# Attention and a two-layer network: item counts per group from a table, operand sums behind the next maximum, a reordered tail

## The chip, the cores and the metric

The kernel runs on one core of a Trainium2 chip. Inputs and outputs lie in the chip's main memory. The metric is the device time of one execution in microseconds (us). A profile of one execution is taken beside it; TensorE ran at its full granted clock in it (1.0).

## The reference

Eight batches, twelve heads, 448 positions, head size 64; then a network of width 768 and inner width 2048. In short:

```python
q_n, k_n = rmsnorm(q, g_q), rmsnorm(k, g_k)          # over the head size
scores = matmul(q_n, k_n^T) / sqrt(64)
attn = exp(scores - max); attn = attn / (sum(attn) + 1e-9)
x = matmul(attn, v)      # -> (8*448, 768)
h = x @ w_in             # (768, 2048)
g = maximum(0.01*h, h)
out = g @ w_out          # (2048, 768)
```

## The kernel before, in words

**Units and quarters.** Attention is cut into 24 units (`u` = 0 to 23): one batch and four of its heads, so three units make a batch. From unit 3 on the main loop has four quarters in each unit (`d` = 0 to 3). A quarter begins with the scores of one or two of the seven key tiles (`qk`, line 199; tile 0 in quarter 0, two tiles in the others) and their exponential on ScalarE (`ex`, line 218). Then `fill(u, d, jobs)` issues some items of the network, which are held in a list `queue`, and the quarter's jobs (loads, squares, normalisation of a later unit, products).

**The head of a unit.** In quarter 0, after the scores of tile 0, VectorE takes their maximum (line 236) and puts it on a diagonal (`dg`, line 238). TensorE does the values product of the unit before (`pv`, line 367, 28 matmuls), its row sums (`zcol`, line 307, 16 to 28 matmuls) and a small matmul that spreads the maxima over the partitions (`shift_mm`, line 248). A second maximum on VectorE (line 249) and line 257 give the bias `eb` of the exponential. ScalarE then copies the values product out (`x`, line 322) and takes the exponential of tile 0. Scores and values product share two slots of PSUM (`sT`): the scores of quarter 1 go into the slot that the exponential of tile 0 has read, and the values product goes into the slot of the last tile of the unit before, after its exponential.

**The row sums' way.** The row sums' logarithm and its exponential (lines 327 and 332) give the reciprocals `zs`, which four transfers on SP's queue spread (`rz`, line 337). The product `xt` of `x` and `rz` (line 347) is made by VectorE in some units and by GpSimd in others (8, 9, 12, 14, 15, 18, 20, 21, 22).

**The network.** `push(b)` adds the items of batch `b` to `queue` once its attention is nearly done. `moe1` is one block of 128 inner columns, six matmuls (line 389), with the activation on ScalarE into `gt` (line 383). The second layer has plain items (`moe2`, line 430: 16 inner blocks into one bank, in two parts of eight matmuls, for half the columns of a tile) and items that make two tiles at once from seven products instead of eight (`seven`, items `i0` to `i6`, line 471, eight matmuls of 384 columns each). The seven products need sums of blocks of `gt` (`s1` to `s4`, lines 452 to 461, into `sa`) and of the weights (`tw`). Their banks are called `ma`, `mb`, `mc`, `md`; merges on VectorE (lines 478 and 487) and copies on ScalarE (line 498) put them together, and `i5` and `i6` add a second product to `mc` and `md`. In batches 6 and 7 part of the first layer is made with seven products too (`late1`, lines 591 to 608).

**What is put off.** An item puts the work on its result into the list `pend` (by `later`), and the next item, or the end of `fill`, issues it (`flush`). So the order of each engine's instructions is written by hand, but for the number of items in each quarter: `fill` works that out from costs of items (`queue[i][0]`) and weights of quarters (`WD`), with the rest carried over in `debt`. After each item one job is issued.

**The tail.** After unit 23 come its row sums and values product, the reciprocals (lines 353 and 354) and two products `xt` (line 376), one for each half `r`; then the rest of the items, among them all of batch 7's. VectorE's order there comes from `pend` too.

Of the kernel before, what the change touches and what calls it, by code (L numbers as in the profile page):

```python
# [18 lines left out]
def kernel(  # L19
# [13 lines left out]
    B, H, S, D = q.shape  # L33
# [378 lines left out]
    pend = []  # L412
    L, R, LR = slice(0, HC), slice(HC, DM), slice(0, DM)

    def flush():
        while pend:
            pend.pop(0)()

    def out_tile():
        return opool.tile([P, DM], FP32, tag="ost", name="ost")  # L420

    def moe2(pair, t, half, part):
        flush()
        if half == 0 and part == 0:
            ost[0] = out_tile()
        if part == 0:
            ost[1] = aux([P, 512], FP32, "op2")
        op2 = ost[1]
        for ft in range(8 * part, 8 * part + 8):
            nc.tensor.matmul(op2[:, 0:HC], gt[:, ft, ds(col(t), P)], wout16[:, ft, ds(HC * half, HC)],  # L430
                             start=(ft == 0), stop=(ft == FT - 1))
        if part == 0:
            return
        nc.vector.tensor_copy(ost[0][:, ds(HC * half, HC)], op2[:, 0:HC])
        drop(op2)
        if half == 1:
            store(pair, t, ost[0], LR, False)

    def wblock(i, j):
        return wout16[:, HF * i:HF * i + HF, HC * j:HC * j + HC]  # L440
# [7 lines left out]
    def gblock(t, j):  # L448
        return gt[:, HF * j:HF * j + HF, ds(col(t), P)]
# [11 lines left out]
        nc.vector.tensor_tensor(sa[:, 3, x], gblock(tt[0], 1)[:, x], sa[:, 1, x], op=ALU.subtract)  # L461

    def later(fn, *args):
        pend.append(lambda: fn(*args))

    def seven(pair, tt, nxt=None, last=False):
        g = {}

        def mm(bank, a, b, first):
            for f in range(HF):  # L470
                nc.tensor.matmul(bank[:, 0:HC], a[:, f], b[:, f], start=(first and f == 0), stop=(f == HF - 1), skip_group_check=not first)  # L471

        def bank(name):
            g[name] = aux([P, 512], FP32, name)
            return g[name]

        def add(dst, src, name):
            nc.vector.tensor_tensor(dst, g[name][:, 0:HC], src, op=ALU.add)

        def put(i, c):  # L480
            store(pair, tt[i], g["o"][i], c, last)

        def i0():
            flush()
            g["o"] = (out_tile(), out_tile())
            mm(bank("ma"), gblock(tt[0], 0), wblock(0, 0), True)
            later(lambda: nc.vector.tensor_copy(g["o"][1][:, L], g["ma"][:, 0:HC]))

        def i1():
            flush()  # L490
            mm(bank("mb"), sa[:, 1], tw[:, 1], True)
            later(lambda: add(g["o"][1][:, L], g["o"][1][:, L], "mb"))
            later(lambda: drop(g["mb"]))

        def i2():
            flush()
            mm(g["ma"], gblock(tt[0], 1), wblock(1, 0), False)
            later(lambda: nc.scalar.copy(g["o"][0][:, L], g["ma"][:, 0:HC]))
            later(lambda: drop(g["ma"]))
            if last:  # L500
                later(put, 0, L)

        def i3():
            flush()
            mm(bank("mc"), sa[:, 0], tw[:, 0], True)
            later(lambda: add(g["o"][1][:, R], g["o"][1][:, L], "mc"))
            if nxt:
                later(s1, nxt)

        def i4():  # L510
            flush()
            mm(bank("md"), sa[:, 2], tw[:, 2], True)
            later(lambda: add(g["o"][1][:, R], g["o"][1][:, R], "md"))
            if last:
                later(put, 1, R)

        def i5():
            flush()
            mm(g["mc"], sa[:, 3], wblock(1, 1), False)
            if nxt:  # L520
                later(s2, nxt)
            later(lambda: add(g["o"][0][:, R], g["o"][1][:, L], "mc"))
            later(lambda: drop(g["mc"]))
            later(put, 0, R if last else LR)
            if nxt:
                later(s3, nxt)
                later(s4, nxt)

        def i6():
            flush()  # L530
            mm(g["md"], gblock(tt[1], 1), tw[:, 3], False)
            later(lambda: add(g["o"][1][:, L], g["o"][1][:, L], "md"))
            later(lambda: drop(g["md"]))
            later(put, 1, L if last else LR)

        return [i0, i1, i2, i3, i4, i5, i6]
# [42 lines left out]
    def late1(b, tail, after):  # L579
# [45 lines left out]
        def item(n, s):  # L625
            flush()
            if not g:
                start()
            if n == 1:
                mm(get(1, s), 1, s, x_b(b, 0, 0), True)  # L630
                later(lambda: copy(tmp["u"][:, s % 2], g[1, s][:, 0:S]))
            elif n == 2:
                mm(get(2, s), 2, s, x_b(b, 1, 0), True)
                later(lambda: vadd(tmp["u"][:, s % 2], g[2, s], tmp["u"][:, s % 2]))
                later(lambda: drop(g[2, s]))
                later(lambda: out_(s, 0, 0, tmp["u"][:, s % 2]))
            elif n == 7:
                mm(get(7, s), 7, s, xs[3], True)
                later(lambda: nc.vector.tensor_copy(tmp["v"][:, s % 2], g[7, s][:, 0:S]))
            elif n == 6:  # L640
                mm(g[1, s], 6, s, xs[2], False)
                later(lambda: vadd(g[7, s][:, 0:S], g[1, s], tmp["v"][:, s % 2]))
            elif n == 5:
                mm(g[1, s], 5, s, xs[1], False)
                later(lambda: vadd(tmp["v"][:, s % 2], g[1, s], tmp["v"][:, s % 2]))
                later(lambda: out_(s, 1, 1, tmp["v"][:, s % 2]))
            elif n == 4:
                mm(g[7, s], 4, s, xs[4], False)
                later(lambda: out_(s, 1, 0, g[7, s][:, 0:S]))
                later(lambda: drop(g[7, s]))  # L650
            else:
                mm(g[1, s], 3, s, x_b(b, 1, 1), False)
                later(lambda: out_(s, 0, 1, g[1, s][:, 0:S]))
                later(lambda: drop(g[1, s]))
            for fn in after.get((n, s), ()):
                pend.append(fn)

        return item

# [14 lines left out]
    def push(b):  # L674
# [24 lines left out]
                    items.append((0.575, lambda w=w: item(*w)))  # L699
        if odd:  # L700
            tt, tn = (3, 4), (5, 6)
            items += [(1.31, fn) for fn in seven(pair, tt, tn)]
            for n, x, fs in ((len(items) - 7, 1, (s3, s4)),) if late else ((8, 0, (s1, s2)), (10, 0, (s3, s4)), (FT - 1, 1, (s1, s2)), (FT, 1, (s3, s4))):
                c, fn = items[n]
                items[n] = (c, also(fn, *[lambda f=f, x=x: later(f, tt, half[x]) for f in fs]))
            items += [(1.31, fn) for fn in seven(pair, tn, None, b == B - 1)]
        else:
            tiles = (2,) if fast else (0, 1, 2)
            std = [lambda t=t, h=h, p=p: moe2(pair, t, h, p) for t in tiles for h in range(2) for p in range(2)]
            if fast:  # L710
                tt = (0, 1)
                std[0] = also(std[0], lambda: later(s1, tt), *[lambda: later(win_sum, 3, 0)] * late)
                std[1] = also(std[1], lambda: later(s2, tt))
                std[2] = also(std[2], lambda: later(s3, tt), lambda: later(s4, tt))
                std += seven(pair, tt)
            items += [(1.31, fn) for fn in std]
        queue.extend(items)

    WD = (3.6, 2.9, 2.8, 2.8)
    STEPS = ((0,), (1, 2), (3, 4), (5, 6))  # L720
    debt = [0.0]

    def narrow(u):
        return 4 <= u < NU - 1
# [1 line left out]
    def fed(u, d):  # L726
        return u % NQ == 0 and d == 3

    def fill(u, d, jobs):
        total = sum(c for c, _ in queue)  # L730
        left = WD[d] + 3.0
        uu, dd = u, d
        while True:
            dd += 1
            if dd == 4:
                uu, dd = uu + 1, 0
            if uu == NU or (fed(uu, dd) and (u > 3 or uu > 3)):
                break
            left += WD[dd]
        debt[0] += total * WD[d] / left  # L740
        while queue and debt[0] >= queue[0][0] * 0.5:
            c, fn = queue.pop(0)
            fn()
            debt[0] -= c
            if jobs:
                jobs.pop(0)()
        flush()
        for job in jobs:
            job()

# [20 lines left out]
    with tc.manual_schedule():  # L771
# [190 lines left out]
        for u in range(3, NU):  # L962
            for d in range(4):
                if d > 0 or u > 3:
                    qk(u, STEPS[d])
                    if d == 0:
                        shift_max(u)
                        if u == 6:
                            xmul_sb(u - 2)
                        if narrow(u - 1):  # L970
# [82 lines left out]
        zsum_slot(NU - 1)  # L1053
        pv(NU - 1)
        zinv(NU - 1)
        xmul(NU - 1)
        for i, ns in enumerate(((3, 1), (2, 4))):
            c, fn = queue[i]
            queue[i] = (c, also(fn, *[lambda n=n: later(x_sum, B - 1, n) for n in ns]))
        push(B - 1)  # L1060
        while queue:
            queue.pop(0)[1]()
# [29 lines left out]
```

## Time and profile before

| | us |
|---|---|
| median of 3 runs | 417.51 (416.79 to 417.85) |
| the profiled execution | 417.04 |
| its span | 415.2 |
| TensorE matmuls busy (3817) | 399.3 |
| VectorE busy | 307.7 |
| ScalarE busy | 300.7 |
| GpSimd busy | 68.4 |

A line of the timeline gives start and duration in us, the engine, the line of the kernel, the operation, output and input, and how many like it follow each other. In square brackets stand the idle time of the engine before it and what ended it. PE is TensorE, DVE VectorE, ACT ScalarE, POOL GpSimd, SP the queue of transfers. A line of the waits gives who waited for whom, the total, how often, and the longest.

### The profile page before, as it was taken

The page shows a single profiled execution, that of the slowest core. Times are in us where ns is not written, and L with a number is a line of the kernel's source. Part 1 is how long each engine was busy: PE and PEld are TensorE (multiplying, and loading weights), DVE is VectorE, ACT ScalarE, POOL GpSimd, SP SyncE. Part 2 cuts the span into 40 slices and gives each one's busy share as a digit, 9 for nine tenths or more (in the row PEclk, how much of TensorE's full clock was granted, in tenths as well). Part 3 has the DMA queues.
Part 4 walks back from the last instruction along what each step waited for, and adds up shares of the span by engine and source line. Part 5 has one row for each costly group of instructions (what it writes and reads, how often), then busy time and mean ns, then how long its engine had stood idle before and what let it go on. Part 6 is the DMA issues. An engine that isn't in the chain of part 4 may idle for free.

```text
span 415.2 us, 9343 instructions
## 1 busy us (share of the span) xinstructions
PE 399.3 (96%) x3817; PEld 219.1 (53%) x3817; DVE 307.7 (74%) x492; ACT 300.7 (72%) x470; POOL 68.4 (16%) x70
## 2 busy tenths in 40 slices
PE   8688999999999999999999999999999999999995
PEld 7444444554445544554445544454445557558863
DVE  5888898898788757867669757767669788557762
ACT  5898887677987699867987679867986657653600
POOL 1868432200020200010020200020001202000000
PEclk9999999999999999999999999999999999999999
DMA  6999999999565986678664896678552460032023
GB/s 207 259 255 253 240 249 141 229 174 207 138 154 92 224 213 125 150 173 182 155 155 72 220 196 136 170 147 185 158 103 47 120 160 8 10 75 77 2 55 98
DMA packets 71950, 62.41 MB, mean 150 GB/s; under 512 B 36324, under 2 KB 67044, under 8 KB 71908
## 3 DMA queue, kind: packets, MB, share of 16 engines
q1 hardware_dynamic: 61312, 49.62, 47.3%
q0 software_dynamic: 10272, 11.80, 18.3%
q8 instruction: 30, 0.49, 0.5%
q10 hardware_dynamic: 324, 0.39, 0.3%
q14 instruction: 12, 0.10, 0.1%
HBM read 45.61 MB, written 11.01 MB: 136 GB/s over the span
## 4 chain that ended last, share of the span: by engine, by line
PE 82%; DVE 9%; ACT 6%; issue 2%; DVEq 0%
PE hps L389 27%; PE sT L199 8%; PE sT L367 5%; PE ma L471 5%; PE op L430 5%; PE md L471 5%; PE bank L591 4%; PE mc L471 4%; PE bank L471 4%; ACT et L218 3%; PE mb L471 3%; PE zc L307 2%; DVE n L171 2%; PE warm L769 2%; PE sT L471 2%
## 5 line engine op out<-in xcount | busy, mean ns | idle before, releaser
L218 ACT ACTIVATE et<-sT,eb 128x896 f16<-128x896 f32 x166 | 159.4, 1008 | 26.7 <-PE sT L199 17.4
L389 PE MATMUL hps<-xt,win 128*128 128x448 f16 x600 | 121.0, 353 | 0.3 <-DVE xt L376 0.2
L389 PEld LDWEIGHTS <-win 128*128 128x128 f16 x612 | 56.8, 98 | 58.4 <-issue 10.0
L383 ACT ACTIVATE gt<-hps 128x448 f16<-128x448 f32 x100 | 53.9, 554 | 7.4 <-PE hps L389 6.4
L199 PE MATMUL sT<-qkT 64*64 64x448 f16 x664 | 52.5, 363 | 4.2 <-ACT et L218 2.8
L159 DVE TENSOR_REDUCE ssq<-sq 128x14 f32<-128x896 f32 (+2 forms) x49 | 50.1, 1059 | 0.6 <-ACT sq L148 0.6
L471 PEld LDWEIGHTS <-sa 128*128 128x128 f16 x352 | 32.8, 98 | 26.3 <-issue 6.1
L128 POOL DMA_DIRECT2D vt<-in_v_dram x24 | 17.9, 746 | 172.0 <-PE sT L367 165.2
L471 PEld LDWEIGHTS <-gt 128*128 128x128 f16 x264 | 25.2, 98 | 19.3 <-issue 2.8
L199 PEld LDWEIGHTS <-qkT 64*64 64x64 f16 x672 | 15.4, 104 | 37.3 <-issue 32.6
L322 ACT COPY x<-sT 128x896 f32<-128x896 f32 x16 | 14.5, 906 | 26.0 <-DVE sT L249 26.0
L347 POOL TENSOR_TENSOR xt<-x,rz 128x896 f16<-128x896 f32 x9 | 18.9, 2097 | 80.3 <-DMA rz<-zs 80.3
L171 DVE TENSOR_TENSOR n<-rq,rinv 128x896 f16<-128x896 f32 (+2 forms) x25 | 27.0, 1084 | 5.0 <-ACT rinv L165 5.0
L292 DVE TENSOR_TENSOR ea<-ea,et 128x896 f16<-128x896 f16 x27 | 16.9, 625 | 16.7 <-ACT et L218 15.7
L367 PE MATMUL sT<-et,vt 64*64 64x448 f16 x532 | 28.5, 349 | 0.3
L430 PE MATMUL op<-wout,gt 128*128 128x384 f16 x160 | 28.4, 326 | 0.0
L236 DVE TENSOR_REDUCE sT<-sT 128x1 f32<-128x896 f32 x22 | 24.1, 1094 | 3.6 <-PE sT L199 3.5
L367 PEld LDWEIGHTS <-vt 64*64 64x64 f16 x672 | 20.5, 107 | 11.3 <-issue 1.4
L171 DVE TENSOR_TENSOR n<-rk,rinv 128x896 f16<-128x896 f32 (+2 forms) x26 | 26.1, 1012 | 0.0
L430 PEld LDWEIGHTS <-gt 128*128 128x128 f16 x192 | 17.6, 98 | 14.4 <-issue 3.1
L471 PE MATMUL ma<-wout,gt 128*128 128x384 f16 x128 | 23.5, 326 | 0.0
L292 DVE TENSOR_TENSOR ea<-et 128x896 f16<-128x896 f16 x14 | 9.4, 673 | 11.8 <-ACT et L218 11.7
(144 smaller groups left out, 549.0 us busy)
## 6 DMA issues: line engine op xcount, KB each, us to landing
rq<-in_q_dram SPq DMA_DIRECT2D x24, 448.0 KB, 4.0
rk<-in_k_dram SPq DMA_DIRECT2D x24, 448.0 KB, 5.5
out_dram<-ost SPq DMA_DIRECT2D x52, 192.0 KB, 3.1
rz<-zs SPq DMA_DIRECT2D x76, 112.0 KB, 2.3
vt<-in_v_dram POOLq DMA_DIRECT2D x24, 224.0 KB, 4.8
win<-in_moe_w_in_dram POOLq DMA_DIRECT2D x8, 384.0 KB, 15.8
wout<-in_moe_w_out_dram POOLq DMA_DIRECT2D x2, 1536.0 KB, 28.9
out_dram<-ost SPq DMA_DIRECT2D x4, 96.0 KB, 2.1
```

The costliest lines, as they stand in the source:

```text
L159: nc.vector.tensor_reduce(buf(u, "ssq")[:, ti, :, c[0]:c[1]], buf(u, f"sq{ti}")[:, :, c[0]:c[1]], axis=AXL.X, op=ALU.add)
L171: nc.vector.tensor_tensor(buf(u, "n16")[:, ti, c[0]:c[1]].rearrange("p s a d -> p a s d"), src[:, :, c[0]:c[1]], buf(u, "rinv")[:, ti, :, ...
L199: nc.tensor.matmul(banks[a][64 * r:64 * r + 64, 0:S].rearrange("p (t x) -> p t x", t=NS), kT(u, r, a, t), qT(u, r, a), start=True, stop=True)
L218: nc.scalar.activation(s["et"][:, t], sT[:, :, 0:S], AF.Exp, bias=s["eb"], scale=1.0)
L236: nc.vector.tensor_reduce(s["spare"][:, 511:512], sT[:, :, 0:S], axis=AXL.XY, op=ALU.max)
L292: nc.vector.tensor_tensor(s["ea"], s["et"][:, 0] if t == 1 else s["ea"], s["et"][:, t], op=ALU.add)
L347: eng.tensor_tensor(xts[b][:, g], s["x32"], s["rz"], op=ALU.mult)
L367: nc.tensor.matmul(s["pv"][r][64 * a:64 * a + 64, 0:S], vts[u % NV][64 * r:64 * r + 64, a, t], s["et"][64 * r:64 * r + 64, t, a], start=(t ...
L383: nc.scalar.activation(dst, src, AF.Prelu, bias=0.0, scale=1.0, alpha=0.01)
L389: nc.tensor.matmul(hps[:, 0:S], win16[:, kt // 2, kt % 2, ts(ft, P)], xt[:, kt // 2, kt % 2], start=(kt == 0), stop=(kt == KT - 1))
L430: nc.tensor.matmul(op2[:, 0:HC], gt[:, ft, ds(col(t), P)], wout16[:, ft, ds(HC * half, HC)], start=(ft == 0), stop=(ft == FT - 1))
L471: nc.tensor.matmul(bank[:, 0:HC], a[:, f], b[:, f], start=(first and f == 0), stop=(f == HF - 1), skip_group_check=not first)
```

## The change

1. `fill` takes the number of items in each quarter from a table, `PLAN`, one row of four digits for each unit from 3 on. The numbers are those that the costs gave before but for three places: quarter 3 of units 11, 15 and 17 has two items where it had one, and quarter 0 of units 12, 16 and 18 has two where it had three.
2. `flush(keep=True)` at the end of a unit leaves `s1` to `s4` in `pend` if they wait there. A new `flush()` behind `shift_max` in quarter 0 issues them. In the built program `s3` and `s4` now stand between the diagonal (line 238) and the second maximum (line 249): with 1024 elements a partition in units 12 and 18, where they stood behind the second maximum; with 512 in units 8, 14 and 20, where they stood ahead of the first.
3. In quarter 2 no job follows item `i4` directly. VectorE does the merge of `md` ahead of the two normalisations of the quarter, in units 9, 12, 15, 18 and 21; it stood between them.
4. `moe2` of batch 6 takes its 16 inner blocks in another order, with 6 and 7 last.
5. In the first `seven` of batch 7, `i0` does six matmuls of `ma`, four of `mb`, and then the last two of `ma`; `i1` does the other four of `mb`.
6. In the tail the product `xt` for `r = 1` is put off behind a merge, and the differences `x_sum` follow it.

In SP's queue the two output stores of the plain item stand ahead of the four `rz` transfers in units 12 and 18, where they stood behind them; in unit 16 two stores of a merge do so too. No instruction is added or removed on any engine.

```diff
@@ -412,23 +412,28 @@
     pend = []
     L, R, LR = slice(0, HC), slice(HC, DM), slice(0, DM)
 
-    def flush():
-        while pend:
-            pend.pop(0)()
+    def flush(keep=False):
+        kept = [p for p in pend if keep and p[0] in (s1, s2, s3, s4)]
+        now = [p for p in pend if p not in kept]
+        pend[:] = kept
+        for fn, args in now:
+            fn(*args)
 
     def out_tile():
         return opool.tile([P, DM], FP32, tag="ost", name="ost")
 
-    def moe2(pair, t, half, part):
+    def moe2(pair, t, half, part, late=False):
         flush()
         if half == 0 and part == 0:
             ost[0] = out_tile()
         if part == 0:
             ost[1] = aux([P, 512], FP32, "op2")
         op2 = ost[1]
-        for ft in range(8 * part, 8 * part + 8):
+        fts = (0, 1, 2, 3, 4, 5, 8, 9, 10, 12, 13, 11, 14, 15, 6, 7) if late else range(FT)
+        for i in range(8 * part, 8 * part + 8):
+            ft = fts[i]
             nc.tensor.matmul(op2[:, 0:HC], gt[:, ft, ds(col(t), P)], wout16[:, ft, ds(HC * half, HC)],
-                             start=(ft == 0), stop=(ft == FT - 1))
+                             start=(i == 0), stop=(i == FT - 1))
         if part == 0:
             return
         nc.vector.tensor_copy(ost[0][:, ds(HC * half, HC)], op2[:, 0:HC])
@@ -461,13 +466,13 @@
         nc.vector.tensor_tensor(sa[:, 3, x], gblock(tt[0], 1)[:, x], sa[:, 1, x], op=ALU.subtract)
 
     def later(fn, *args):
-        pend.append(lambda: fn(*args))
-
-    def seven(pair, tt, nxt=None, last=False):
+        pend.append((fn, args))
+
+    def seven(pair, tt, nxt=None, last=False, mixed=False):
         g = {}
 
-        def mm(bank, a, b, first):
-            for f in range(HF):
+        def mm(bank, a, b, first, fs=range(HF)):
+            for f in fs:
                 nc.tensor.matmul(bank[:, 0:HC], a[:, f], b[:, f], start=(first and f == 0), stop=(f == HF - 1), skip_group_check=not first)
 
         def bank(name):
@@ -483,12 +488,16 @@
         def i0():
             flush()
             g["o"] = (out_tile(), out_tile())
-            mm(bank("ma"), gblock(tt[0], 0), wblock(0, 0), True)
+            ma = bank("ma")
+            if mixed:
+                mm(ma, gblock(tt[0], 0), wblock(0, 0), True, range(6))
+                mm(bank("mb"), sa[:, 1], tw[:, 1], True, range(4))
+            mm(ma, gblock(tt[0], 0), wblock(0, 0), True, range(6 if mixed else 0, HF))
             later(lambda: nc.vector.tensor_copy(g["o"][1][:, L], g["ma"][:, 0:HC]))
 
         def i1():
             flush()
-            mm(bank("mb"), sa[:, 1], tw[:, 1], True)
+            mm(g["mb"] if mixed else bank("mb"), sa[:, 1], tw[:, 1], True, range(4 if mixed else 0, HF))
             later(lambda: add(g["o"][1][:, L], g["o"][1][:, L], "mb"))
             later(lambda: drop(g["mb"]))
 
@@ -513,6 +522,8 @@
             later(lambda: add(g["o"][1][:, R], g["o"][1][:, R], "md"))
             if last:
                 later(put, 1, R)
+
+        i4.merges = True
 
         def i5():
             flush()
@@ -653,7 +664,7 @@
                 later(lambda: out_(s, 0, 1, g[1, s][:, 0:S]))
                 later(lambda: drop(g[1, s]))
             for fn in after.get((n, s), ()):
-                pend.append(fn)
+                later(fn)
 
         return item
 
@@ -699,14 +710,14 @@
                     items.append((0.575, lambda w=w: item(*w)))
         if odd:
             tt, tn = (3, 4), (5, 6)
-            items += [(1.31, fn) for fn in seven(pair, tt, tn)]
+            items += [(1.31, fn) for fn in seven(pair, tt, tn, mixed=late)]
             for n, x, fs in ((len(items) - 7, 1, (s3, s4)),) if late else ((8, 0, (s1, s2)), (10, 0, (s3, s4)), (FT - 1, 1, (s1, s2)), (FT, 1, (s3, s4))):
                 c, fn = items[n]
                 items[n] = (c, also(fn, *[lambda f=f, x=x: later(f, tt, half[x]) for f in fs]))
             items += [(1.31, fn) for fn in seven(pair, tn, None, b == B - 1)]
         else:
             tiles = (2,) if fast else (0, 1, 2)
-            std = [lambda t=t, h=h, p=p: moe2(pair, t, h, p) for t in tiles for h in range(2) for p in range(2)]
+            std = [lambda t=t, h=h, p=p: moe2(pair, t, h, p, late) for t in tiles for h in range(2) for p in range(2)]
             if fast:
                 tt = (0, 1)
                 std[0] = also(std[0], lambda: later(s1, tt), *[lambda: later(win_sum, 3, 0)] * late)
@@ -716,9 +727,10 @@
             items += [(1.31, fn) for fn in std]
         queue.extend(items)
 
-    WD = (3.6, 2.9, 2.8, 2.8)
+    PLAN = ("2212", "2212", "2112", "2122", "3232", "3322", "2322",
+            "2322", "3232", "2222", "3323", "3232", "2322", "2322",
+            "3232", "2222", "3323", "3232", "2322", "4356", "5232")
     STEPS = ((0,), (1, 2), (3, 4), (5, 6))
-    debt = [0.0]
 
     def narrow(u):
         return 4 <= u < NU - 1
@@ -727,24 +739,12 @@
         return u % NQ == 0 and d == 3
 
     def fill(u, d, jobs):
-        total = sum(c for c, _ in queue)
-        left = WD[d] + 3.0
-        uu, dd = u, d
-        while True:
-            dd += 1
-            if dd == 4:
-                uu, dd = uu + 1, 0
-            if uu == NU or (fed(uu, dd) and (u > 3 or uu > 3)):
-                break
-            left += WD[dd]
-        debt[0] += total * WD[d] / left
-        while queue and debt[0] >= queue[0][0] * 0.5:
-            c, fn = queue.pop(0)
+        for n in range(int(PLAN[u - 3][d])):
+            fn = queue.pop(0)[1]
             fn()
-            debt[0] -= c
-            if jobs:
+            if jobs and not (d == 2 and hasattr(fn, "merges")):
                 jobs.pop(0)()
-        flush()
+        flush(keep=d == 3 and u < NU - 1)
         for job in jobs:
             job()
 
@@ -965,6 +965,7 @@
                     qk(u, STEPS[d])
                     if d == 0:
                         shift_max(u)
+                        flush()
                         if u == 6:
                             xmul_sb(u - 2)
                         if narrow(u - 1):
@@ -1053,10 +1054,10 @@
         zsum_slot(NU - 1)
         pv(NU - 1)
         zinv(NU - 1)
-        xmul(NU - 1)
-        for i, ns in enumerate(((3, 1), (2, 4))):
+        xmul(NU - 1, (0,))
+        for i, more in enumerate((((xmul, NU - 1, (1,)), (x_sum, B - 1, 3), (x_sum, B - 1, 1)), ((x_sum, B - 1, 2), (x_sum, B - 1, 4)))):
             c, fn = queue[i]
-            queue[i] = (c, also(fn, *[lambda n=n: later(x_sum, B - 1, n) for n in ns]))
+            queue[i] = (c, also(fn, *[lambda m=m: later(*m) for m in more]))
         push(B - 1)
         while queue:
             queue.pop(0)[1]()
```

## The prediction

> **What bounds the kernel now.** I read the page's busy times first, then what ended TensorE's idle time, then the timeline around each place that the edit touches.
>
> ```profile
> PE 399.3 (96%) x3817; PEld 219.1 (53%) x3817; DVE 307.7 (74%) x492; ACT 300.7 (72%) x470; POOL 68.4 (16%) x70
> ```
>
> TensorE is busy 399.3 of 415.2 us. The first 66 us of start-up hold 9.6 of the idle and the last store 4.2, so from 66 to 411 us little is left, and the edit removes no matmul. TensorE's waits from 40 us on:
>
> ```profile
> PE sT L248 <- DVE dg L238: 0.5, 3, 0.2
> PE bank L430 <- ACT gt L601: 0.5, 1, 0.5
> PE bank L471 <- ACT gt L601: 0.2, 1, 0.2
> ```
>
> A recorded matmul end is a model, so I measure holes from start to start against the same sequence undisturbed. The head of unit 12, then that of unit 9, in the timeline:
>
> ```profile
> 172.11 0.38 PE L199 MATMUL sT<-qkT 64*64 64x448 f16 x4
> 172.59 1.52 PE L367 MATMUL sT<-et,vt 64*64 64x448 f16 x28
> 172.69 0.68 DVE L455 TENSOR_TENSOR sa<-sa,gt 128x1024 f16<-128x1024 f16 x1
> 173.29 1.09 DVE L236 TENSOR_REDUCE sT<-sT 128x1 f32<-128x896 f32 x1
> 174.76 0.22 PE L248 MATMUL sT<-dg,onesp 128*128 128x64 f16 x2 [0.15 <-DVE dg L238]
> ...
> 126.89 0.38 PE L199 MATMUL sT<-qkT 64*64 64x448 f16 x4
> 129.12 0.23 PE L248 MATMUL sT<-dg,onesp 128*128 128x64 f16 x2
> 130.58 1.01 ACT L218 ACTIVATE et<-sT,eb 128x896 f16<-128x896 f32 x1
> 131.88 0.57 PE L199 MATMUL sT<-qkT 64*64 64x448 f16 x8
> ```
>
> Unit 12 takes 2.65 us from score to shift matmul; unit 8, with the same 16 row-sum matmuls, takes 2.13 (110.59 to 112.72). The hole is 0.52: the values product waits for the last exponential (172.54), then the maximum is late behind s2. In unit 9 the exponential frees the score slot at 131.59, 0.29 before the next scores want it. Unit 12's merge, and the tail:
>
> ```profile
> 183.79 2.07 POOL L347 TENSOR_TENSOR xt<-x,rz 128x896 f16<-128x896 f32 x1 [8.66 <-DMA rz<-zs]
> 184.90 1.92 DVE L171 TENSOR_TENSOR n<-rq,rinv 128x896 f16<-128x896 f32 x1 [0.31 <-ACT rinv L165]
> 186.74 0.55 DVE L478 TENSOR_TENSOR ost<-md,ost 128x384 f32<-128x384 f32 x1
> 187.34 1.46 PE L471 MATMUL md<-tw,gt 128*128 128x384 f16 x8
> ...
> 356.97 1.14 PE L430 MATMUL bank<-wout,gt 128*128 128x384 f16 x6
> 358.58 0.50 PE L430 MATMUL bank<-wout,gt 128*128 128x384 f16 x2 [0.47 <-ACT gt L601]
> ...
> 373.26 1.46 PE L471 MATMUL bank<-wout,sa 128*128 128x384 f16 x8
> 374.80 1.46 PE L471 MATMUL bank<-tw,gt 128*128 128x384 f16 x8
> ```
>
> The last merge product starts late because the merge it overwrites stood behind the q normalisation, itself held by GpSimd. The 1.61 and 1.54 between starts in the tail should be 0.98 and 1.30: eight 384-column matmuls start every 1.30 us (404.28 to 405.58), 0.163 each.
>
> **What the Trainium skill says.** "Perfetto Trace Analysis", section Tensor Engine Instruction: TensorE's end times are estimated, and VectorE and ScalarE run strictly in order. The trace agrees: the last hole shows as 0.14 idle between 185.73+1.47 and 187.34, but as 0.31 by starts. "SBUF — State Buffer", section Who interferes with whom: a VectorE operation with two SBUF inputs is shut out while GpSimd reads SBUF, one with a single SBUF input is not. It agrees: the normalisation took 1.92 instead of 1.09 under GpSimd's product, while a PSUM merge at 184.03 took its usual 0.56. "DMA: Bandwidth & Descriptors", section Issuing engines are not separate DMA queues: all transfers share 16 engines. No run here separates that yet.
>
> **The change, part by part.** Q is the start of a unit's first scores.
>
> *Table.* It repeats the old planner's item counts except for one 8-matmul item each, drawn from unit 12 into 11, 16 into 15, 18 into 17. Work is equal; cover moves ahead of the head. Unit 12: +1.30 before Q puts scores at 173.4, after the exponential (172.54) and after s2 (173.37). The maximum then starts at Q+0.50 and the diagonal ends at Q+1.93, as in unit 8, before the shift matmul at Q+2.13. Gain 0.52; unit 18, with the same 2.65, also 0.52. Unit 16 takes 2.72 against unit 13's 2.42 with 28 row sums (its product waited for the exponential of 235.08+1.91); the moved item covers that: 0.30. Its new head still has two six-matmul products, 2.43 us, as unit 10 has without a hole.
>
> *Sums behind the maximum.* In 12 and 18 s3 and s4 (0.68 each, one start every 0.60) now stand between diagonal and second maximum. They start at about Q+1.85, so the second maximum starts at Q+3.05 instead of Q+2.40. Queued behind it: the bias, ScalarE's copy, the exponential. From maximum to exponential is 1.15 (270.35 to 271.49), and the exponential takes 1.01: the score slot is free at Q+5.21. With one item fewer after the shift, the next scores want it at Q+4.89 (unit 9: 2.76 after the shift). New stall 0.32 each, from 0.28 to 0.37 by how exactly the slot's end is read. Net 0.20 per unit, 0.40 for both. In units 8, 14, 20 the halves (0.42, spaced 0.34) delay the maximum by 0.15; 1.1 us of slack at the slot covers that, else it would cost 0.15.
>
> *Merge before normalisation* (units 9, 12, 15, 18, 21). The last-but-one merge no longer waits for the normalisation: unit 12's 0.31 goes. Elsewhere it gains nothing. The k normalisation ends about 0.45 later; the following merge waited 0.61 for TensorE anyway (283.88). Without that cover the next maximum would be 0.45 late, about its slack. The SP transpose behind it also starts 0.45 later; unit 16's VectorE already waits 0.70 for one (242.10), but nothing on TensorE needs it for a unit.
>
> *Stores.* In units 12 and 18 two output stores pass in front of the four reciprocal transfers in SP's queue. The copy they await ends near Q+4.26; their two issues took 1.25 (unit 18) and 2.41 (unit 12). The reciprocal is ready at about Q+5.9, now Q+5.74, so SP is free in time in the first case, 0.8 late in the second. GpSimd's product follows 4.4 (273.19 to 277.55) to 5.9 us later (177.85 to 183.79), and holds the q normalisation to its end. Counting two normalisations (2.0) and two merges after that end, against the next maximum's usual place (scores at Q+14.8, plus 0.58) and a slack of 0.5 behind it, TensorE is delayed only if the product ends after Q+12.94. I expect Q+12.4 to 13.6: nothing for 18, 0.10 charged for 12; the ends are 0 and 0.66 each. Loads behind the stores have units of slack. Unit 16's store likewise passes its reciprocals; with VectorE taking that product (249.14) there is slack.
>
> *Tail.* Columns 6 and 7 are taken last, and 8 to 15 were written by 358.09: 1.61−0.98 = 0.63. The split reciprocal product lets the merge run between its halves: 1.54−1.30 = 0.24; the second half, 0.5 later, is needed only two items on. The mixed products: six matmuls from 392.20, then four of mb, then the last two without their 0.37 hole; but mb's second half needs s2, done at 394.41, so it ends at 395.11 instead of 395.18: 0.07. What follows is TensorE-bound to 410.9, and ScalarE and VectorE wait for it there, so the 0.94 stays.
>
> Sum: 0.40+0.30+0.31+0.94−0.10 = 1.85. The profiled execution took 417.04 us (415.2 span, 1.8 around it): 415.2. Against the median of the runs, 417.51, it is 415.7, −0.44%.
>
> **Rivals.** (1) *Tail only.* Head stalls of 0.52 instead of 0.32 and late products eat the 1.0 of the middle. For: the score slot's slack was only 0.29 in unit 9. Against: the starts above. 417.51−0.94 = 416.6. (2) *No new stall.* The two sums fit between diagonal and shift, or the slot comes free earlier (unit 10's scores started 0.04 before the recorded exponential end): 0.64 more, 414.9 rounded with no product loss. (3) *Slower: the product of GpSimd.* Both stores take 2.41, from Q+4.3 to 6.7; reciprocals start 0.96 late, unit 12's product at Q+12.64, ending Q+14.71, 1.77 past the limit. In 12 and 18: 3.54−1.95 = 1.6 slower, 419.1. It decides from an end of Q+13.92 (twice 0.98). For: it overlaps even now. Against: unit 18's product runs 1.6 earlier. (4) *Nothing arrives:* the holes are replaced by others in the same unit, 417.5.
>
> **Numbers.** Likeliest 0.50 (own range 415.2 to 416.2), tail only 0.25, no new stall 0.10, slower 0.08, nothing 0.07. Range 414.9 to 416.9: it leaves out the slower case and the edges. Faster by over 0.3% (1.25 us, about what a measurement of this kernel can tell from no change) 0.60: most of the likeliest, the no-stall case, a little of tail-only. Within 0.3% 0.28; slower 0.12, with an edge from the neighbours of (3).
>
> **What would show it.** In the profile after: score to shift 2.13 in units 12 and 18, 2.42 in 16; L199 there waiting for ACT about 0.3; the late merge's product 1.30 after the one before; the split item of the tail followed at 1.30; the first matmul gone from the waits of L430. I am wrong if the maximum of units 13 or 19 starts more than a microsecond after its scores, or a new wait of 0.5 us stands anywhere else on TensorE.

## The result and the profile after

The changed kernel took 416.12 us (median of 4 runs, 415.62 to 416.56), the kernel before 417.30 beside it (4 runs). The ratio is 0.9971, with a 95% interval of 0.9951 to 0.9992. A second comparison, with more runs, gave 415.77 against 416.92, ratio 0.9975 (0.9968 to 0.9983): 1.0 to 1.2 us faster. The profiled execution took 415.69 us, its span 413.9.

The busy times of the changed kernel, from its page:

```profile
PE 399.0 (96%) x3817; PEld 219.0 (53%) x3817; DVE 308.1 (74%) x492; ACT 300.3 (73%) x470; POOL 68.4 (17%) x70
```

The work is the same. What TensorE waited for from 40 us on, in the waits of the changed kernel (who waited for whom, total, times, longest):

```profile
PE sT L248 <- DVE dg L238: 0.5, 1, 0.5
PE sT L476 <- DVE sa L460: 0.2, 1, 0.2
```

Four more lines, of 0.2 to 0.7 us, stand in both kernels with the same numbers and are left out here and in the prediction. The three waits for the diagonal have become one, and the two for ScalarE's activations into `gt` are gone. The wait for the diagonal that is left is a new one: 0.5 us, in unit 13. The other line is the forecast rest of edit 5: the second half of `mb`, at 393.26, waits for `s2`, which ends at 393.20.

The head of unit 12 in the timeline of the changed kernel, and the scores of its second quarter with the weight loads (PEld) ahead of them:

```profile
173.86 0.38 PE L199 MATMUL sT<-qkT 64*64 64x448 f16 x4
174.36 1.10 DVE L236 TENSOR_REDUCE sT<-sT 128x1 f32<-128x896 f32 x1 [0.54 <-PE sT L199]
175.70 0.68 DVE L463 TENSOR_TENSOR sa<-gt 128x1024 f16<-128x1024 f16 x1
175.99 0.23 PE L248 MATMUL sT<-dg,onesp 128*128 128x64 f16 x2
176.90 0.29 DVE L249 TENSOR_REDUCE sT<-sT 128x1 f32<-128x128 f32 x1
178.03 1.01 ACT L218 ACTIVATE et<-sT,eb 128x896 f16<-128x896 f32 x1
178.75 0.14 PEld L199 LDWEIGHTS <-qkT 64*64 64x64 f16 x5 [0.32 <-issue]
179.10 0.11 PEld L199 LDWEIGHTS <-qkT 64*64 64x64 f16 x3 [0.21 <-issue]
179.41 1.09 PEld L476 LDWEIGHTS <-sa 128*128 128x128 f16 x8 [0.20 <-issue]
```

From the scores to the shift matmul it is now 2.13 us (2.65 before); the maximum starts 0.50 after the scores. The second maximum comes at 3.04 after the scores, behind the two sums; it came at 2.90 in this unit before, and comes at 2.40 where neither a late maximum nor sums are in its way (unit 8 before). The scores of the next quarter start on time, 4.89 after the first, but only their first tile, whose four matmuls have all started by 178.85; those of the second tile start from 179.10 on, when the exponential has ended (178.03+1.01). The next item follows 0.66 after these scores instead of 0.51, so the new stall is 0.15.

Unit 12's merges and the head of unit 13:

```profile
184.98 2.08 POOL L347 TENSOR_TENSOR xt<-x,rz 128x896 f16<-128x896 f32 x1 [8.38 <-ACT rinv L165]
185.43 0.56 DVE L483 TENSOR_TENSOR ost<-md,ost 128x384 f32<-128x384 f32 x1 [0.74 <-PE md L476]
185.83 1.47 PE L476 MATMUL mc<-wout,sa 128*128 128x384 f16 x8
185.91 2.10 DVE L171 TENSOR_TENSOR n<-rq,rinv 128x896 f16<-128x896 f32 x1
187.14 1.46 PE L476 MATMUL md<-tw,gt 128*128 128x384 f16 x8
188.53 0.38 PE L199 MATMUL sT<-qkT 64*64 64x448 f16 x4
190.06 1.09 DVE L236 TENSOR_REDUCE sT<-sT 128x1 f32<-128x896 f32 x1
191.52 0.22 PE L248 MATMUL sT<-dg,onesp 128*128 128x64 f16 x2 [0.49 <-DVE dg L238]
```

The last merge product now follows at 1.31 us (1.61 before): its hole is closed, and the merge runs at its usual 0.56 under GpSimd's product. But the q normalisation starts at 185.91 and ends at 188.01, 0.95 after GpSimd (187.06). Everything behind it on VectorE moves on, the maximum of unit 13 starts 1.53 after its scores, and the shift matmul comes at 2.99 instead of 2.42. So 0.57 is given back at once. GpSimd's product itself is not later than it was: it starts 11.12 after the scores of its unit, against 11.68 before. But the unit is one item shorter, 14.67 against 16.62, so the next scores come sooner behind it.

The tail of the changed kernel:

```profile
356.51 1.46 PE L435 MATMUL bank<-wout,gt 128*128 128x384 f16 x8
357.90 0.57 PE L199 MATMUL sT<-qkT 64*64 64x448 f16 x8
...
372.16 1.46 PE L476 MATMUL bank<-wout,sa 128*128 128x384 f16 x8
373.46 1.46 PE L476 MATMUL bank<-tw,gt 128*128 128x384 f16 x8
...
375.91 0.74 PE L602 MATMUL bank<-xs,win 128*128 128x224 f16 x6
376.02 0.55 DVE L483 TENSOR_TENSOR ost<-bank,ost 128x384 f32<-128x384 f32 x1
376.62 0.73 PE L602 MATMUL bank<-xt,win 128*128 128x224 f16 x6
```

From the plain item to the scores behind it: 1.39 (2.04 before). Between the last two merge products: 1.30 (1.54). A small hole is new: the first-layer product at 376.62 starts 0.71 after the one before, where 0.57 is usual (377.25 to 377.82 in the kernel before). By the starts it waits for a bank that the last merge (376.02+0.55) frees, though the waits name no cause. That merge stands behind two differences of `x_sum`, as it did before, when TensorE came later and it was done in time. The 0.71 stands in all nine profiles with the tail's edits, the 0.57 in all five without.

### The profile page after: what moved, and what is told of

Its sections match the earlier page's. It is cut to its first block, busy times and chain, and to the rows that moved or that the text cites. A ratio compares the mean times of both kernels' runs of the same rounds, so it can differ in the third digit from the quotient of the medians.

```text
span 413.9 us, 9346 instructions
## 1 busy us (share of the span) xinstructions
PE 399.0 (96%) x3817; PEld 219.0 (53%) x3817; DVE 308.1 (74%) x492; ACT 300.3 (73%) x470; POOL 68.4 (17%) x70
## 4 chain that ended last, share of the span: by engine, by line
PE 84%; DVE 9%; ACT 4%; issue 1%; DMA 1%; SPq 0%; DVEq 0%
PE hps L389 27%; PE sT L199 8%; PE sT L367 6%; PE ma L476 5%; PE mc L476 5%; PE op L435 5%; PE bank L602 5%; PE bank L476 5%; PE md L476 5%; DVE n L171 3%; PE mb L476 3%; PE zc L307 3%; ACT et L218 2%; PE sT L476 1%; PE bank L435 1%
```

## The experiments

Two sums are compared throughout. One is from the first scores of unit 5 to those of unit 23, the middle; the other from there to the last group of matmuls, the tail. Both are free of the start-up, whose first scores came anywhere from 9.68 to 10.45 us in these profiles, in part by when the first block of k landed (its square starts at 5.15 to 5.89). One chance is left in the middle: unit 21 took 15.92 us in some profiles and up to 16.37 in others, 16.16 and 15.92 in the two of before, 15.92 and 16.18 in the two of the changed kernel; the last section tells why.

| kernel | middle, us | tail, us | ratio to before (95%) |
|---|---|---|---|
| before, two profiles | 283.06, 282.56 | 57.67, 57.68 | |
| changed, two profiles | 282.15, 282.49 | 56.87, 56.87 | 0.9975 (0.9968 to 0.9983) |
| tail only | 282.76 | 56.88 | 0.9982 (0.9974 to 0.9991) |
| middle only | 282.48 | 57.68 | 0.9989 (0.9978 to 0.9999) |
| table only | 283.67 | 57.67 | 1.0026 (1.0018 to 1.0034) |
| merge only | 282.51 | 57.68 | 0.9999 (0.9986 to 1.0011) |
| changed, merge as before | 283.61 | 56.88 | 1.0004 (0.9995 to 1.0013) |
| changed, sums at the unit's end | 282.10 | 56.88 | 0.9981 (0.9971 to 0.9992) |
| changed, sums behind the bias | 282.33 | 56.88 | 0.9969 (0.9958 to 0.9980) |
| changed, stores behind the reciprocals | 281.72 | 56.87 | 0.9975 (0.9958 to 0.9991) |
| both mends, two profiles | 281.49, 281.54 | 56.88, 56.87 | 0.9950 (0.9937 to 0.9963) |

**The changed kernel again, and the kernel before against itself.** Neither has an edit.

> The changed kernel once more, beside the kernel before on the same chip. Ledger theory (the sum of the holes between TensorE's starts, from unit 5 to the end: +0.68 in unit 12, -0.55 in unit 13, +0.29 in 16, +0.35 in 18, -0.06 in 19, +0.24 in 21, about +0.85 in the tail = 1.8 us): with the start-up alike on both sides, 1.8 us faster, ratio 0.9957. Rival (the start-up of the changed kernel is 0.45 us longer for a reason in the change): 1.3 us faster, ratio 0.9968, and the first scores again 0.45 us later than before.

> The kernel before against itself, as a control. In the profiles so far the first scores come at 9.68 to 9.77 us in the three kernels without the table and at 9.72 to 10.45 in the ten with it, though the instructions up to there are the same. If the later start belongs to the programs with the table: first scores at 9.7 again. If it is luck of the first load of k: anywhere from 9.7 to 10.4. Ratio 1.000 within the interval. Unit 12's shift matmul 2.65 us after its scores, unit 18's 2.65, unit 16's 2.72 again; unit 21's by where GpSimd's product of unit 20 starts: 2.23 if before 10.47 us after the scores, later by as much as it is later.

Measured: 415.77 us against 416.92, 1.15 faster and so nearer to the rival's 1.3 than to the 1.8 of the ledger; and for the control 417.02 against 416.71, ratio 1.0009 (0.9995 to 1.0023), so 0.1 to 0.2% is what such a comparison can be off by. The start-up of the changed kernel was again late (first scores at 10.29); that of the control came at 9.87, between the two expectations. Whether the programs with the table start later is left open: with it the first scores came at 9.72 to 10.45, without it at 9.68 to 9.87, over the same instructions. The middle and the tail of the changed kernel are 1.4 to 1.7 us shorter than in the first profile of before, 0.9 to 1.2 shorter than in the control's; the times say 1.0 to 1.2. The heads of the control repeat: 2.65, 2.65 and 2.72 in units 12, 18 and 16. Two things do not. The hole at unit 12's last merge product is 0.05 there instead of 0.31, with GpSimd's product 0.25 earlier. And unit 21's shift matmul comes at 2.23 instead of 2.48. Both hang on when GpSimd's product starts, and that varies from run to run.

**The tail alone, and the middle alone.** The first is the kernel before with edits 4 to 6, the second the changed kernel without them:

```diff
-        fts = (0, 1, 2, 3, 4, 5, 8, 9, 10, 12, 13, 11, 14, 15, 6, 7) if late else range(FT)
+        fts = range(FT)
-            items += [(1.31, fn) for fn in seven(pair, tt, tn, mixed=late)]
+            items += [(1.31, fn) for fn in seven(pair, tt, tn)]
-        xmul(NU - 1, (0,))
+        xmul(NU - 1)
...
```

In the last place the put-off half of the product goes out of the list behind it as well.

> Only the three edits of the tail, on the kernel before. Ledger theory: 0.63 for the order of the inner blocks, 0.24 for the split reciprocal product, about 0.05 for the mixed products: 0.9 us faster, ratio 0.998. Rival (the middle carries all, the tail's end is set by ScalarE's chain): within 0.3 us of before.

> Only the table, the kept sums and the merge before the normalisation; the tail as before. Ledger theory: 0.9 us faster (1.8 less 0.9), shift matmul of unit 13 at 2.9 to 3.0 us after its scores. Rival 'tail only' of the prediction: within 0.3 us of before.

Measured: 416.34 and 416.54 us against 416.92; ratios 0.9982 and 0.9989. The tail is 0.80 shorter wherever its edits are in, and nowhere else. The middle alone gives 0.4 by the times, half of what was expected, and by its sum 0.1 to 0.6, depending on which profile of before is taken (its shift matmul of unit 13 stands at 3.11). The whole change is 0.57 faster than the tail alone (415.77 against 416.34, 22 runs each). So the rival 'tail only' falls, but only just: resampling these 44 times gives 0.1 to 0.9 for the 0.57 (95%), and by the sums 0.80 of the gain is the tail's.

**The table alone.** The kernel before with `PLAN` in `fill`, and nothing else.

> Only the table, on the kernel before; sums, merges and tail as before. Ledger theory: with one item fewer before the merges, GpSimd's product falls on the q normalisation, and the last merge product of units 12 and 18 waits for both: unit 12 0.3 to 0.6 longer than in the kernel before (next scores 15.32 after its own, the moved item taken off), unit 18 0.3 to 0.4 longer; unit 16 0.3 shorter: 0.3 to 0.8 us slower than before, ratio 1.001 to 1.002. Rival (the table is where the gain comes from, the other edits are small): 0.7 to 1.3 faster than before, ratio 0.997 to 0.998.

Measured: 418.05 us against 416.87, ratio 1.0026 (1.0018 to 1.0034): slower. The timeline of unit 12 shows why:

```profile
184.79 2.08 POOL L347 TENSOR_TENSOR xt<-x,rz 128x896 f16<-128x896 f32 x1 [8.19 <-ACT et L218]
185.25 2.56 DVE L171 TENSOR_TENSOR n<-rq,rinv 128x896 f16<-128x896 f32 x1 [0.31 <-ACT rinv L165]
186.08 1.47 PE L476 MATMUL mc<-wout,sa 128*128 128x384 f16 x8
187.74 0.54 DVE L483 TENSOR_TENSOR ost<-md,ost 128x384 f32<-128x384 f32 x1
188.33 1.46 PE L476 MATMUL md<-tw,gt 128*128 128x384 f16 x8 [0.78 <-DVE ost L483]
```

With one item fewer in the unit the q normalisation falls under GpSimd's product. The merge behind it is late, and the last product follows at 2.25 instead of 1.31. Unit 12 is 15.86 long, unit 18 15.62, where the kernel before has 16.62 and 16.33 with one item of 1.30 more, so they lose 0.54 and 0.59. Unit 16 gains its 0.3. By these sums the table pays only with the merge ahead of the normalisation.

**The merge before the normalisation, taken out and alone.** Out of the changed kernel, and alone in the kernel before:

```diff
-            if jobs and not (d == 2 and hasattr(fn, "merges")):
+            if jobs:
```

> The changed kernel with the merge of the last-but-one product again between the two normalisations of the quarter. Ledger theory: GpSimd's product now lies over the q normalisation in units 12 and 18, so the merge comes only after it: the last merge product of unit 12 starts about 2.7 us after the one before instead of 1.31, that of unit 18 about 2.2; in turn unit 13's maximum is no longer late (0.57 back). About 1.7 us slower than the changed kernel, no faster than before. Rival (this edit was worth the 0.31 of the old hole and no more): 0.3 us slower than the changed kernel.

> Only the merge ahead of the normalisations, on the kernel before. Ledger theory: the hole of 0.31 ahead of unit 12's last merge product goes, nothing else moves, unit 13's shift matmul stays at 2.42: 0.3 us faster, ratio 0.999, which the interval may not tell from no change. Rival (the late normalisation makes the next maximum late here too): unit 13's shift matmul later than 2.5, no gain.

Measured: without it 417.08 us against 417.00, ratio 1.0004, some 1.2 slower than the changed kernel where 1.7 was expected; the last product follows at 2.57 in unit 12 and 2.08 in unit 18, and unit 13's shift matmul is at 2.43 again. So in the changed kernel the edit is worth 1.1 to 1.5 us of the middle (283.61 against 282.15 and 282.49), not the old hole of 0.31. Alone it closes that hole (1.31) and its time cannot be told from no change (0.9999).

**Where the sums stand.** At the unit's end, ahead of the next first maximum; and behind the bias:

```diff
-        flush(keep=d == 3 and u < NU - 1)
+        flush()
-                        flush()
```
```diff
                         shift_max(u)
-                        flush()
...
                             shift_mm(u)
+                            flush()
```

> The changed kernel with the sums issued at the end of the unit, ahead of the next first maximum. Ledger theory: in units 12 and 18 the maximum starts about 1.08 us after the scores instead of 0.50, the shift matmul at 2.5 to 2.6 instead of 2.13 (0.4 lost each), and the stall of 0.15 at the slot goes: about 0.5 us slower than the changed kernel. Rival (where the sums stand does not matter, the gain is the table's): within 0.2 us of the changed kernel.

> The changed kernel with the kept sums behind the bias instead of ahead of the second maximum; stores stay ahead of the reciprocals. Theory A (the second maximum, 0.64 us late behind the sums, makes the reciprocals and so GpSimd's product late): second maximum of unit 12 at 2.40 us after its scores, the stall of 0.15 at the scores of its second quarter gone, product about 0.4 us earlier (10.7 us after the scores instead of 11.1), unit 13's shift matmul at 2.5 to 2.6; 0.6 to 0.8 us faster than the changed kernel. Theory B (the stores ahead of the reciprocals make the product late): product at 11.1, unit 13 at 2.9 to 3.0; only 0.3 faster.

Measured: 416.12 and 415.73 us against 417.00; ratios 0.9981 and 0.9969. At the unit's end the shift matmuls of units 12 and 18 come at 2.55, as expected, but the middle is 282.10, no longer than in the changed kernel: the slot's stall is gone, and unit 13's shift is at 2.50, since the unit is longer (14.93 against 14.67) and the product of GpSimd falls earlier in it. The 0.5 us that edit 2 was expected to be worth is not seen in either measure: as it was placed, it bought nothing that can be told from zero. Behind the bias, the second maximum is at 2.40 and both stalls of 0.15 are gone, but unit 13 stays at 2.92. SP's queue in unit 12, whose first scores stand at 173.43:

```profile
178.03 1.17 SPq L409 DMA_DIRECT2D out_dram<-ost  x2
179.36 3.00 SPq L337 DMA_DIRECT2D rz<-zs  x4
```

The reciprocals were ready at 5.23 after the scores, 0.6 earlier than in the changed kernel, and were issued at 5.93, no earlier, since SP was busy with the two stores until 5.77. Theory A is not wrong, but the stores hid it.

**The stores behind the reciprocals, and both mends together.**

```diff
-            store(pair, t, ost[0], LR, False)
+            if pair:
+                later(store, pair, t, ost[0], LR, False)
+            else:
+                store(pair, t, ost[0], LR, False)
```

> The changed kernel with the plain item's stores behind the four reciprocal transfers; the kept sums stay ahead of the second maximum. Theory B (stores): the four transfers are issued in 2.5 us instead of 3.3 and land without the stores' 384 KB, GpSimd's product of unit 12 starts at 10.3 us after the scores instead of 11.1, unit 13's shift matmul at 2.4 to 2.5; 0.5 to 0.6 us faster than the changed kernel, the two stalls of 0.15 stay. Theory A (second maximum): product at 11.0 or later, unit 13 at 2.9 to 3.0; no change of time.

> The changed kernel with the kept sums issued behind the bias of unit 12 and 18 instead of ahead of the second maximum, and with the plain item's stores behind the four reciprocal transfers on SP's queue. Theory (the new stall at the score slot and the late product of GpSimd are what the change gives back, and both follow from these two places): the stalls of 0.15 in units 12 and 18 go, the shift matmul of unit 13 comes 2.42 us after its scores instead of 2.99 and that of unit 19 at 2.42 instead of 2.50; 0.9 to 1.0 us faster than the changed kernel, some 2.7 faster than before. Rival (the late product comes from the unit being one item shorter, whatever SP and the second maximum do): unit 13 stays at 2.9 to 3.0, 0.3 us faster than the changed kernel.

> The version with both mends once more, for a narrower interval. By the starts of the first profile it takes 281.5 us from the first scores of unit 5 to those of unit 23, the changed kernel 282.2 and 282.5, the kernel before 283.1; with the tail's 0.9 that is 2.4 us faster than before and 0.7 to 1.0 faster than the changed kernel: ratio 0.994 to 0.9957 against before. Rival (start-up differences carried the first time): no faster than the changed kernel's 0.9972.

With the stores behind, the reciprocals of unit 12 are issued as in the changed kernel (5.89 after the scores) but GpSimd's product starts at 10.65 (10.3 was expected) instead of 11.00 to 11.26, and unit 13's shift matmul comes at 2.51. Theory B holds in its effect, but not because SP is blocked: in the changed kernel the stores are issued by 5.47, before the reciprocals are ready at 5.86. So the transfers are issued at the same time and their data are used later with the stores in flight. For unit 12 this is one profile, in a way that varies much from run to run (last section); unit 18 shows the same, 10.27 against 10.49 to 10.64. The middle is 281.72, while the time, 415.85 against 417.00, does not show it over the changed kernel (0.9958 to 0.9991, 7 runs).

With both mends, some 2.7 us less than before was expected. Measured: 415.15 against 416.92, ratio 0.9957 (0.9942 to 0.9973), and the second time 414.91 against 416.87, ratio 0.9950 (0.9937 to 0.9963). Around the head of unit 13 in the profile of that second time:

```profile
184.09 2.07 POOL L347 TENSOR_TENSOR xt<-x,rz 128x896 f16<-128x896 f32 x1 [7.76 <-ACT et L218]
185.48 1.63 DVE L171 TENSOR_TENSOR n<-rq,rinv 128x896 f16<-128x896 f32 x1
188.11 0.38 PE L199 MATMUL sT<-qkT 64*64 64x448 f16 x4
190.62 0.22 PE L248 MATMUL sT<-dg,onesp 128*128 128x64 f16 x2
```

The reciprocals go out at 5.24, the product starts at 10.50 (10.27 the first time), the shift matmul is at 2.51 (2.42). This is the version to keep: 1.8 to 2.0 us faster than the kernel before, and 0.6 faster than the changed kernel beside it (415.15 against 415.77). The rival, that the shorter unit keeps the shift matmul at 2.9 to 3.0 whatever SP and the second maximum do, falls. The shorter unit is still the condition: in the kernel before the product started later, at 11.43 and 11.68, and did no harm.

## Why the prediction was right, and where it was not

415.7 us was forecast and 416.12 measured, inside 414.9 to 416.9. The gain was off by more: 1.85 us (0.44%) was forecast, 1.2 (0.29%) measured. The places and the causes were mostly right, the sizes were not, and that the total came this near is in part luck: the new stall cost 0.30 in all instead of 0.64, while the stores, charged with 0.10, cost 0.6 to 0.7. Two of the prediction's own signs of being wrong came true: the maximum of unit 13 starts 1.53 and 1.66 after its scores in the two profiles (that of unit 19 1.04 and 0.90), and a new wait of 0.5 us stands in unit 13. By the steps:

- *Table, heads of 12, 16 and 18.* 0.52, 0.30 and 0.52 forecast; the shift matmuls came at 2.13, 2.43 and 2.14 after the scores, as forecast (0.52, 0.29, 0.51). Right.
- *Sums behind the maximum, "net 0.20 per unit".* The mechanism was right to the second maximum (3.05 forecast, 3.04 measured). The stall was 0.15, not 0.32. The slot was the mistake, in the description of the kernel too: the four matmuls of the first score tile start by 178.85, before the exponential ends at 179.04, so that tile does not go into the slot that the exponential reads. It takes the other, that of the values product, free since ScalarE's copy ended at 178.14. Only the second tile waits for the exponential, and it wants the slot four score matmuls later.
- *Merge before normalisation, "unit 12's 0.31 goes; elsewhere it gains nothing".* The hole went. But 0.31 was the size of one run (0.05 in the other profile of the kernel before), and what the edit is worth beside the table is 1.1 to 1.5, because with the table in, the normalisation ahead of the merge falls under GpSimd's product. I costed the two edits one by one against the old trace and missed that they need each other; the sum was right as both are in.
- *Stores, "0.10 charged for 12".* The mis-sized term of the sum: 0.57 and 0.70 in unit 13 (two profiles), 0.08 and 0.01 in unit 19. The mechanism is the one described, GpSimd holding the q normalisation. The limit for the product's end was put at Q+12.94; it is Q+12.63, since the next scores came at 14.67 instead of 14.8, the head's slack is 0.12 smaller than I took, and the work after the product 0.06 longer. And the product ended at 13.20 and 13.34, inside the range of 12.4 to 13.6 but above the 13.0 that the charge meant.
- *Tail, 0.94.* 0.80: 0.65 for the order of the inner blocks, 0.24 for the split product and 0.06 for the mixed products, as forecast to 0.02, less the new hole of 0.14 behind the last merge. "What follows is TensorE-bound" was wrong for that one item.

With the measured sizes the sum is 0.52+0.29+0.51 − 2×0.15 + 0.31 − 0.63 − 0.04 + 0.80 = 1.46. (The sums of the first two profiles give 1.7; 0.24 of that is unit 21's chance.) Taking the merge's hole at 0.05 to 0.31, it is 1.2 to 1.5, against 1.0 to 1.2 by the times. What is left, up to 0.5, is within what the control and the start-up can be off by, and was not settled.

## What to carry to other kernels

An edit that takes work out of one stage moves every later operation of that stage against transfers and engines that do not move with it: look up what the shortened stage will now run into, and cost edits in pairs, as one may be worth nothing or less alone. Measure holes of a full engine between starts, against the same sequence undisturbed. Before a filler is put into a gap of a critical chain, check that what is behind it has slack; here the place behind the chain's last link was better.

## What the runs showed of the hardware

A VectorE operation with two inputs in SBUF that runs into GpSimd's product does not end before the product does. In the fourteen profiles 22 q normalisations overlap a product of GpSimd in units 12 and 18: each ends 0.94 to 0.96 us after the product's end, whenever it started, so that they take 1.19 to 2.88 where 1.09 is usual. A sum of 512 elements, 0.42 alone, took 1.75 and 1.99 in unit 20 (changed and before). A merge with one input in PSUM kept its 0.56. So unit 21's shift matmul follows the start of unit 20's product: it comes 2.23 after its scores if that product starts up to 10.33 after the scores of its unit, at 2.25 for 10.47, 2.35 for 10.59, 2.48 for 10.71, 2.51 for 10.74 and 2.69 for 10.91, from 10.59 on one for one. The two profiles of before stand at 10.71 and 10.31, so that this chance of 0.25 needs no edit.

In unit 18, from the first issue of the reciprocals to the product it took 4.36 to 4.44 us in all seven profiles with the two 192 KB stores behind them, and 4.61 to 4.75 in all seven with them ahead: two stores whose issue ends 0.2 to 0.4 us earlier still lengthen these transfers. The Trainium skill's "DMA: Bandwidth & Descriptors", section Issuing engines are not separate DMA queues, has all transfers share 16 engines. This is in line with it but no test of it, as stores and reciprocals both go through SP's queue here. In unit 12 the same way took 4.8 to 6.1, with the stores on either side; what lengthens it there was not found.
